# Seven PSUM banks shared with the side work in halved lumps, and a gelu whose VectorE instruction reads one SBUF operand

## The chip, the cores and the metric

The kernel runs on one core of a Trainium2 chip. The metric is the device time of one execution in microseconds, the median of the runs shown; lower is better. PE is TensorE, ACT ScalarE, DVE VectorE, POOL GpSimd; PEld is TensorE's weight load.

## What is computed

An adaLN block: 2048 tokens of width 512, 32 heads of width 16, then a token-shift MLP and a channel MLP with 1792 hidden columns. All in fp32.

```
h = layernorm(x) * (1 + ca) + sa
x = x + ga * (softmax(q k^T / 4) v) @ wo          # q, k, v = h @ wqkv, 32 heads
h = layernorm(x) * (1 + cb) + sb
t = gelu(layernorm(h) @ w1); t = shift(t, +1, -1, +2, -2 by quarters)
x1 = h + t @ w2
x = x + gb * (x1 + gelu(layernorm(x1) @ w3) @ w4)  # gelu: the tanh form
```

## The kernel before

**Attention is the spine.** There are 64 units, each a pair of heads (j = 0, 1) against one chunk of 512 queries, and 16 steps in a unit, one for each 128 keys. For each half step PE does a row pair: a score matmul (`sc`, L865) and a matmul for the row maximum of a later unit (`mb`, L849), each into a PSUM bank of its own. DVE reduces `mb` to a maximum (L845); ACT takes the exponential of `sc` into the int32 tile `pt` (L861). The exponential is written as an integer whose two 16-bit halves are used as two fp16 numbers. The low half needs a scaling by 0.5, one instruction over 128x1024 for each step (`p_low`): L909 on POOL, and in every eighth step (`LACT`) L907 on ACT. Then PE multiplies by V into `pv` (L924), two matmuls for the high half and two for the low half of each step.

**Blocks.** The rows and columns are written out in blocks of three half steps (`GRP`): six row matmuls, then the six `pv` matmuls of the block two before (`LAG`). So the scaling of a step has about two blocks until PE needs it. The block that finds its banks not yet drained waits on PE.

**Side work.** Between blocks PE does lumps of everything else: in units 0 to 15 the projections of q, k and v, and the splitting of the MLP weights into a high and a low part ("pieces": ACT copies to the high part, L750, DVE subtracts for the low part, L751); in units 16 to 63 the MLP of the 512 tokens that the 16 units before have finished ("tail", three of them beside attention; the fourth runs after it). All fp32 products are three matmuls of high and low parts (L298, L300, L302). A planner, `Sched`, runs while the program is built: it keeps an estimated time for each engine, gives each block a budget of side work, and puts an instruction of a side chain on ACT, DVE or POOL where it sees room. Nothing of it is left on the chip but the order: each engine executes its own list in order and waits for semaphores. `BMAX` caps a lump.

**PSUM.** Eight banks: one for `pv`, six in rotation for `sc` and `mb` (`NSM`), and one, `d0`, for all side work. (Before the main loop three of the six are lent to the side work.)

**The gelu** of the tails (L1187 to L1206) on a bank of 128x256 or 128x128: ACT copies half of the bank to `xs` (L1200) and squares it to `sq` (L1193), which frees the bank; DVE multiplies `(sq + 1/a) * xs` (L1201); ACT takes tanh (L1202); DVE multiplies `(tanh + 1) * xs` (L1203); ACT copies the high part (L1204); POOL subtracts for the low part (L1205). Both DVE instructions read two SBUF tiles. A tail has 36 of them: 8 of w1, 28 of w3.

Of the kernel before, what the change touches and what calls it, by code (L numbers as in the profile page):

```python
# [21 lines left out]
P = 128  # L22
# [18 lines left out]
BMAX = 1600.0  # L41
# [8 lines left out]
NSM = 6  # L50
LEND = 3
LENDS = -4
GRP = 3
LACT = 8
# [14 lines left out]
class Sched:  # L69
# [28 lines left out]
    def chain(self, *ops, prio=1, ready=None, bank=None):  # L98

        if ready is None:  # L100
            ready = self.T["P"] + PX
        n = 0
        while n < len(self.chains) and self.chains[n][2] <= prio:
            n += 1
        self.chains.insert(n, [ready, list(ops), prio, bank is not None and id(bank.tensor)])
# [18 lines left out]
    def misc(self, e, until):  # L124

        while True:
# [11 lines left out]
            ch = best[1]  # L138
            _, cost, fn = ch[1].pop(0)
            self.late = 0.0  # L140
            end = self.put(e, cost, ch[0], fn)
            if ch[1]:
                n = ch[1][0][0]
                ch[0] = max(end + (0 if n == e else XP[e] if n is None else XX), self.late)
            else:
                self.chains.remove(ch)
# [48 lines left out]
    def banks(self, n):  # L195
        self.avail, self.back, self.owner = list(range(n)), [], {}
        self.lent = None

    def return_banks(self, fn):

        self.lent = fn
        for i in self.avail:
            if i:
                fn(i, self.T["P"])
        for i, t in self.back:
            if i:
                fn(i, t)
        self.avail = [i for i in self.avail if not i]
        self.back = [x for x in self.back if not x[0]]

    def take(self, tile):

        i = self.avail.pop(0)
        b = tile(i)
        self.owner[id(b.tensor)] = i
        return b

    def free(self, b):

        i = self.owner.pop(id(b.tensor), None)  # L220
        if i and self.lent:
            self.lent(i, self.end + 200)
        elif i is not None:
            self.back.append((i, self.end + 200))
# [22 lines left out]
class Slots:  # L247
# [22 lines left out]
def kernel(ctx, tc, A_x, A_wqkv, A_wo, B_w1, B_w2, B_w3, B_w4, c, w_mod, out):  # L270
# [81 lines left out]
    def dbank(n):  # L352
        return sch.take(lambda i: psd["d"].tile([P, CH], F32, name=n, tag=f"s{NSM - i}" if i and psd["s"] else f"d{i}", bufs=1))
# [375 lines left out]
    def pieces_gen():  # L729
        while True:  # L730
# [15 lines left out]
            def store(i=i, c=c, w=w, f=f, gone=gone):  # L746
                for h, t in enumerate((w.bitcast(F32), f)):
# [3 lines left out]
                      ("D", cD(), lambda f=f, t=t, w=w: dve.tensor_tensor(t, f, w, op=OP.subtract)),  # L751
# [81 lines left out]
    def max_part(m, j):  # L833
# [6 lines left out]
        ready, sm.t[x] = sm.t[x], 1e9  # L840
# [10 lines left out]
    def score_part(s, j):  # L851
# [5 lines left out]
        ready, sm.t[x] = sm.t[x], 1e9  # L857
        r = slice(64 * j, 64 * j + 64)

        def after(e):  # L860
            ea = sch.crit("A", 500, e + PX, lambda: act.activation(pt[s][:, j], b, AF.Exp))  # L861
# [39 lines left out]
    def p_low(s):  # L901
# [4 lines left out]
        if s % LACT == LACT - 1:  # L906
            e_low[s] = XP["A"] + sch.crit("A", 945, ready, lambda: act.activation(o, i, AF.Copy, scale=0.5))  # L907
# [138 lines left out]
    def tail(ci):  # L1046
# [140 lines left out]
        def gelu(b, n, hi, lo, key):  # L1187
# [8 lines left out]
            def end():  # L1196
                done.add(key)
                live.remove(key)

            sch.chain(("A", cA(n), lambda: act.activation(xs, b, AF.Copy, scale=0.5)), ("A", cA(n), square),  # L1200
# [141 lines left out]
    for k, blk in enumerate(blocks + [[]] * LAG):  # L1342
        if LENDS in blk:
            sch.return_banks(lambda i, t: sm.t.__setitem__(NSM - i, t))
        if 0 in blk:
            while any(sch.owner.values()):
                sch.step()
# [9 lines left out]
        t, start = CIN, 0.0  # L1357
        banks = sorted(sm.t)
# [9 lines left out]
        sch.gap(start)  # L1368
        sch.T["P"] = max(sch.T["P"], start) + CIN
# [20 lines left out]
    while ("att", NC - 1) not in done:  # L1390
        sch.step()
# [41 lines left out]
```

## Time and profile before

| | |
|---|---|
| median of 3 runs | 2235.69 us (2226.3 to 2235.8) |
| the profiled execution, its own time | 2238.01 us |
| its span in the trace | 2236.1 us |
| mean granted clock of TensorE | 0.975 of full speed |
| PE, DVE, ACT, POOL busy | 94%, 80%, 72%, 67% of the span |

Attention begins at about 110 us and ends at about 2068 us; before it lies the first layernorm, behind it the fourth tail. The four stages of 16 units each take some 500 us: the first from 112 to 560 in the windows below, then one tail each. An instruction's "idle before" is time in which its engine had nothing to execute, with what ended it. PE's busy time counts matmuls until their modelled ends, so a PE at 97% can still start a block late.

### The profile page before, as it was taken

The numbers are of one execution on the slowest core, as the hardware profiler recorded it, in microseconds if no ns is written. First come the engines' busy times: TensorE is split into PE (matmuls) and PEld (weight loads), VectorE is DVE, ScalarE is ACT, GpSimd is POOL, SyncE is SP. The second block draws the span as 40 slices with busy tenths as digits, with TensorE's granted clock in tenths as the row PEclk, the third lists the DMA queues.
The fourth block names the chain that finished last, engine by engine and source line by source line (L and its number), as shares of the span: only waits on it lengthen the run. The fifth ranks groups of instructions, "written<-read, shape, count | busy, mean of one in ns | idle before, by whom it ended". The sixth has DMA issues, their size and how long they took to land.

```text
span 2236.1 us, 37341 instructions
## 1 busy us (share of the span) xinstructions
PE 2109.6 (94%) x12400; PEld 1181.3 (53%) x12400; DVE 1785.1 (80%) x3064; ACT 1615.7 (72%) x3254; POOL 1504.0 (67%) x1421
## 2 busy tenths in 40 slices
PE   6889999999999999999999999999899999999799
PEld 5544555554445555554445555555444555554688
DVE  6768887778998888888898888888798888884553
ACT  6467886667877777777868778777677877778353
POOL 3356776568966776667767877677678866768342
PEclk9889999998999999999999999999999999999999
DMA  5788887547644345446343344444524452443332
GB/s 196 197 253 254 218 231 208 154 142 204 178 140 118 113 104 149 112 112 182 75 111 91 98 109 135 126 111 97 163 75 111 112 149 80 126 112 114 132 131 81
DMA packets 201713, 313.37 MB, mean 140 GB/s; under 512 B 85520, under 2 KB 137232, under 8 KB 177296
## 3 DMA queue, kind: packets, MB, share of 16 engines
q1 hardware_dynamic: 201520, 310.98, 49.2%
q8 instruction: 99, 1.62, 0.3%
q14 instruction: 94, 0.77, 0.1%
HBM read 243.27 MB, written 67.11 MB: 139 GB/s over the span
## 4 chain that ended last, share of the span: by engine, by line
PE 59%; DVE 23%; ACT 8%; DMA 4%; issue 3%; POOL 2%; SPq 1%; POOLq 0%; ACTq 0%; DVEq 0%
PE pv L924 15%; DVE mx L845 14%; PE mb L849 10%; PE sc L865 8%; PE w L298 6%; PE w L300 5%; PE w L302 5%; ACT pt L861 3%; ACT pt L907 2%; DVE xs L1203 2%; DVE sq L1201 2%; DMA vst<-Vs 1%; DMA kst<-Ks 1%; DVE tst L309 1%; PE ot L949 1%
## 5 line engine op out<-in xcount | busy, mean ns | idle before, releaser
L909 POOL TENSOR_SCALAR pt<-pt 128x1024 f16<-128x1024 uint16 x896 | 1210.4, 1376 | 436.8 <-ACT pt L861 428.0
L845 DVE TENSOR_REDUCE mx<-mb 128x1 f32<-128x512 f32 x2048 | 1281.3, 681 | 220.9 <-PE mb L849 201.4
L861 ACT ACTIVATE pt<-sc 128x512 int32<-128x512 f32 x2048 | 1082.3, 607 | 272.3 <-PE mb L849 230.1
L849 PE MATMUL mb<-kst,qtl 48*128 48x512 f32 x2048 | 754.3, 457 | 46.8 <-DVE mx L845 27.8
L865 PE MATMUL sc<-qtl,kst 64*128 64x512 f32 x2048 | 726.7, 447 | 8.1 <-DVE mx L845 3.9
L924 PE MATMUL pv<-pt,vst 128*64 128x512 f16 x4096 | 614.2, 403 | 26.9 <-ACT pt L907 13.8
L849 PEld LDWEIGHTS mb<-kst,qtl 48*128 48x128 f32 x2048 | 352.8, 196 | 225.4 <-DVE mx L845 142.0
L865 PEld LDWEIGHTS sc<-qtl,kst 64*128 64x128 f32 x2048 | 339.4, 189 | 160.1 <-ACT pt L861 56.1
L924 PEld LDWEIGHTS <-vst 128*64 128x64 bf16 x4096 | 182.1, 109 | 335.1 <-issue 260.4
L298 PE MATMUL w<-A,wr 128*128 128x256 f32 (+2 forms) x576 | 178.5, 310 | 5.5 <-ACT A L292 3.0
L1205 POOL TENSOR_TENSOR g<-xs,g 128x256 fp32r<-128x256 f32 (+2 forms) x144 | 104.9, 731 | 115.2 <-ACT g L1204 115.0
L907 ACT ACTIVATE pt<-pt 128x1024 f16<-128x1024 uint16 x128 | 175.7, 1373 | 0.0
L300 PE MATMUL w<-A,wr 128*128 128x256 f32 (+2 forms) x576 | 168.4, 292 | 1.5 <-DVE A L288 1.3
L302 PE MATMUL w<-A,wr 128*128 128x256 f32 (+2 forms) x576 | 168.7, 293 | 0.0
L298 PEld LDWEIGHTS w<-A,wr 128*128 128x128 f32 x576 | 110.8, 192 | 56.4 <-ACT pt L861 24.6
L1203 DVE SCALAR_TENSOR_TENSOR xs<-sq,xs 128x256 f32<-128x256 f32 (+2 forms) x144 | 105.1, 734 | 37.6 <-ACT sq L1202 34.3
L1201 DVE SCALAR_TENSOR_TENSOR sq<-sq,xs 128x256 f32<-128x256 f32 (+2 forms) x144 | 110.4, 768 | 20.0 <-ACT sq L1193 18.9
L1200 ACT ACTIVATE xs<-w 128x256 f32<-128x256 f32 (+2 forms) x144 | 55.5, 386 | 92.9 <-PE w L302 92.0
L298 PE MATMUL w<-wr,g 128*128 128x512 f32 x288 | 121.6, 422 | 0.5 <-issue 0.5
L300 PE MATMUL w<-wr,g 128*128 128x512 f32 x288 | 119.1, 414 | 0.0
L302 PE MATMUL w<-wr,g 128*128 128x512 f32 x288 | 117.2, 407 | 0.3 <-POOL g L1205 0.3
L302 PEld LDWEIGHTS w<-A,wr 128*128 128x128 f32 x576 | 111.2, 193 | 9.5 <-issue 9.5
(124 smaller groups left out, 2015.0 us busy)
## 6 DMA issues: line engine op xcount, KB each, us to landing
wr<-Ws SPq DMA_DIRECT2D x80, 1024.0 KB, 5.2
vst<-Vs SPq DMA_DIRECT2D x62, 1024.0 KB, 6.3
kst<-Ks SPq DMA_DIRECT2D x126, 384.0 KB, 6.8
Vs<-vt SPq DMA_DIRECT2D x32, 512.0 KB, 4.9
qtl<-Qs SPq DMA_DIRECT2D x128, 96.0 KB, 4.8
Ws<-wq SPq DMA_DIRECT2D x40, 256.0 KB, 4.4
Ws<-wst SPq DMA_DIRECT2D x40, 256.0 KB, 3.8
wst<-in_B_w_dram SPq DMA_DIRECT2D x36, 256.0 KB, 4.4
```

The source lines that it names most:

```text
L298: te.matmul(o, lh, rh, start=first, stop=False)
L300: te.matmul(o, lh, rl, start=False, stop=False)
L302: te.matmul(o, ll, rh, start=False, stop=last)
L845: end = sch.crit("D", 605, e + PX, lambda: dve.reduce_max(mxs[u][:, j, g, c:c + 1], b, axis=AX.X))
L849: return ready, lambda: te.matmul(b, lhs, kst[u % 3][r, c * CH:(c + 1) * CH], start=True, stop=True), after
L861: ea = sch.crit("A", 500, e + PX, lambda: act.activation(pt[s][:, j], b, AF.Exp))
L865: return ready, lambda: te.matmul(b, kst[u % 3][r, kt * P:(kt + 1) * P], qst[u][r], start=True, stop=True), after
L907: e_low[s] = XP["A"] + sch.crit("A", 945, ready, lambda: act.activation(o, i, AF.Copy, scale=0.5))
L909: e_low[s] = XP["G"] + sch.crit("G", 1345, ready, lambda: pool.tensor_scalar(o, i, 0.5, 1.0, op0=OP.mult, op1=OP.mult))
L924: te.matmul(pv[u][64 * j:64 * j + 64, :], v[:, kt, i, 64 * j:64 * j + 64], p[:, j, 1 - i::2], start=(kt == 0 and i == 0), stop=(kt == NKT ...
L1201: ("D", cD(n), lambda: dve.scalar_tensor_tensor(sq, sq, 1.0 / GELU_A, xs, op0=OP.add, op1=OP.mult)),
L1203: ("D", cD(n), lambda: dve.scalar_tensor_tensor(xs, sq, 1.0, xs, op0=OP.add, op1=OP.mult)),
```

## The change

Four things change.

1. **Banks.** `NSM` is 7: `sc`, `mb` and the side work take any of seven banks (`share`, `take`); `d0` is gone. From unit 0 on the side work may hold two at a time (`MOST`), of which one may still be written (`open`). Ahead of a block `flush` emits the draining chains of banks that the block will need.
2. **Lumps.** `BMAX` falls from 1600 to 800 planned ns. Over the 64 units the PE order has 568 lumps between rows and columns in place of 524.
3. **The gelu** of the first three tails: ACT squares and copies the bank, unscaled; DVE multiplies `(sq + 1/a) * bank`, reading one SBUF tile and the bank, and only then is the bank free; ACT tanh; ACT `0.5 t + 0.5`; POOL multiplies `xs * sq`; then the high and low parts as before. One DVE instruction less, one more on ACT and on POOL. The fourth tail keeps the old gelu.
4. **Who scales and splits.** The pieces' subtraction moves from DVE to POOL (40 instructions of 128x512). The scaling of the low half goes to ACT only where the planner sees POOL over 800 ns behind ACT, and then as two instructions of 128x512: 17 steps of 1024 in place of 128.

The counts in the changed program: the old DVE pair remains 22 times for 128x256 and 14 times for 128x384 (both in the fourth tail); the new DVE instruction stands 94 times for 128x256 and 14 times for 128x128. POOL has 1007 scalings in place of 896.

```diff
-BMAX = 1600.0
+BMAX = 800.0
...
-NSM = 6
-LEND = 3
+NSM = 7
+MOST0 = 4
+MOST = 2
...
-LACT = 8
+LACT = 800.0
...
+    def share(self, slots, most):
+        self.avail, self.back, self.owner = [], [], {}
+        self.slots, self.most = slots, most
     def take(self, tile):
-        i = self.avail.pop(0)
+        if self.slots:
+            i = self.slots.take()
+            self.slots.t[i] = LATE
+        else:
+            i = self.avail.pop(0)
         b = tile(i)
         self.owner[id(b.tensor)] = i
+        self.open = id(b.tensor)
         return b
...
     def room(self, n=1):
+        if self.slots:
+            return self.open is None and len(self.owner) < self.most and min(self.slots.t) <= self.T["P"]
...
+    def flush(self, n):
+        for ch in list(self.chains):
+            while self.slots.late() > len(self.slots.t) - n and ch[1] and ch[3] in self.owner:
+                self.emit(ch)
...
             sch.chain(*ops, ("A", cA(), lambda f=f, w=w: act.activation(w, f, AF.Copy)),
-                      ("D", cD(), lambda f=f, t=t, w=w: dve.tensor_tensor(t, f, w, op=OP.subtract)),
+                      ("G", cG(), lambda f=f, t=t, w=w: pool.tensor_tensor(t, f, w, op=OP.subtract)),
...
-        if s % LACT == LACT - 1:
-            e_low[s] = XP["A"] + sch.crit("A", 945, ready, lambda: act.activation(o, i, AF.Copy, scale=0.5))
+        g, a = [max(sch.T[e], ready) for e in "GA"]
+        if g > a + LACT:
+            for h in range(2):
+                c = slice(h * CH, (h + 1) * CH)
+                e_low[s] = XP["A"] + sch.crit("A", 690, ready, partial(act.activation, o[:, c], i[:, c], AF.Copy, scale=0.5))
...
+            if psd["s"]:
+                def square_copy():
+                    act.activation(sq, b, AF.Square)
+                    act.activation(xs, b, AF.Copy)
+                    sch.T["A"] += cA(n)
+                def cube():
+                    dve.scalar_tensor_tensor(sq, sq, 1.0 / GELU_A, b, op0=OP.add, op1=OP.mult)
+                    sch.free(b)
+                sch.chain(("A", cA(n), square_copy), ("D", cD(n), cube),
+                          ("A", cA(n), lambda: act.activation(sq, sq, AF.Tanh, scale=GELU_A * GELU_C)),
+                          ("A", cA(n), lambda: act.activation(sq, sq, AF.Copy, scale=0.5, bias=0.5)),
+                          ("G", cG(n), lambda: pool.tensor_tensor(xs, xs, sq, op=OP.mult)), *tail_ops, bank=b)
+                return
...
-        if 0 in blk:
-            while any(sch.owner.values()):
-                sch.step()
...
+        need = sum((s >= 0) + (s + LEAD < NS) for s, _ in row)
+        sch.flush(need)
...
         sch.gap(start)
+        sch.flush(need)
```

What stands in the queues, at the first gelus of w3 in the second tail. On DVE, before: L845 is the maximum of a row, L1201 and L1203 are the gelu's two.

```order
L1201 SCALAR_TENSOR_TENSOR sq<-sq,xs 128x256
L845 TENSOR_REDUCE mx<-mb 128x1 x3
L1201 SCALAR_TENSOR_TENSOR sq<-sq,xs 128x256
L1203 SCALAR_TENSOR_TENSOR xs<-sq,xs 128x256 x2
L845 TENSOR_REDUCE mx<-mb 128x1 x5
L1201 SCALAR_TENSOR_TENSOR sq<-sq,xs 128x256
L845 TENSOR_REDUCE mx<-mb 128x1 x3
L1203 SCALAR_TENSOR_TENSOR xs<-sq,xs 128x256
L845 TENSOR_REDUCE mx<-mb 128x1 x3
L1201 SCALAR_TENSOR_TENSOR sq<-sq,xs 128x256
```

On DVE, in the changed kernel, at the same gelus: L863 is the maximum, L1232 the gelu's one, which reads the bank `w`.

```order
L1232 SCALAR_TENSOR_TENSOR sq<-sq,w_16235 128x256
L863 TENSOR_REDUCE mx<-mb 128x1 x8
L1232 SCALAR_TENSOR_TENSOR sq<-sq,w_16318 128x256
L863 TENSOR_REDUCE mx<-mb 128x1 x3
L1232 SCALAR_TENSOR_TENSOR sq<-sq,w_16420 128x256
L863 TENSOR_REDUCE mx<-mb 128x1 x6
L1232 SCALAR_TENSOR_TENSOR sq<-sq,w_16464 128x256
L863 TENSOR_REDUCE mx<-mb 128x1 x3
```

Of the two instructions a gelu one is left, and three to eight maxima stand between one gelu and the next; the old pairs stood back to back in places. On POOL, before: L909 scales a step, L1205 subtracts for a gelu.

```order
L909 TENSOR_SCALAR pt<-pt 128x1024 x4
L1205 TENSOR_TENSOR g_15929<-xs,g_15929 128x256
L909 TENSOR_SCALAR pt<-pt 128x1024 x2
L1205 TENSOR_TENSOR g_15929<-xs,g_15929 128x256 x2
L909 TENSOR_SCALAR pt<-pt 128x1024 x4
L1205 TENSOR_TENSOR g_16274<-xs,g_16274 128x256
```

On POOL, in the changed kernel: L931 scales, L1238 is the gelu's product, L1223 its subtraction.

```order
L931 TENSOR_SCALAR pt<-pt 128x1024 x2
L1223 TENSOR_TENSOR g_16011<-xs,g_16011 128x256
L931 TENSOR_SCALAR pt<-pt 128x1024 x3
L1238 TENSOR_TENSOR xs<-xs,sq 128x256
L931 TENSOR_SCALAR pt<-pt 128x1024
L1223 TENSOR_TENSOR g_16011<-xs,g_16011 128x256
L931 TENSOR_SCALAR pt<-pt 128x1024 x3
L1238 TENSOR_TENSOR xs<-xs,sq 128x256
L931 TENSOR_SCALAR pt<-pt 128x1024
L1223 TENSOR_TENSOR g_16011<-xs,g_16011 128x256
L1238 TENSOR_TENSOR xs<-xs,sq 128x256
```

There a gelu comes to four scalings with two instructions beside them, where it had one beside two to four. On ACT, before, at two gelus a little later in the same tail: L861 is the exponential, L907 the scaling on ACT, L1200, L1193, L1202 and L1204 the gelu's.

```order
L1202 ACTIVATE sq<-sq 128x256
L861 ACTIVATE pt<-sc 128x512 x3
L907 ACTIVATE pt<-pt 128x1024
L1204 ACTIVATE g_16274<-xs 128x256
L1200 ACTIVATE xs<-w_16579 128x256
L1193 ACTIVATE sq<-w_16579 128x256
L861 ACTIVATE pt<-sc 128x512 x3
L1202 ACTIVATE sq<-sq 128x256
L861 ACTIVATE pt<-sc 128x512 x3
L1204 ACTIVATE g_16274<-xs 128x256
```

On ACT, in the changed kernel: L879 is the exponential, L1227, L1228, L1236, L1237 and L1222 the gelu's square, copy, tanh, scaled copy and high part.

```order
L1227 ACTIVATE sq<-w_16589 128x256
L1228 ACTIVATE xs<-w_16589 128x256
L1236 ACTIVATE sq<-sq 128x256
L879 ACTIVATE pt<-sc 128x512 x3
L1237 ACTIVATE sq<-sq 128x256
L879 ACTIVATE pt<-sc 128x512 x3
L1227 ACTIVATE sq<-w_16673 128x256
L1228 ACTIVATE xs<-w_16673 128x256
L1236 ACTIVATE sq<-sq 128x256
L1222 ACTIVATE g_16419<-xs 128x256
L879 ACTIVATE pt<-sc 128x512 x3
```

The long scaling is gone from between the exponentials; the gelu has five short instructions where it had four.

## Rows read from the trace of the kernel before

**Rows 1.** The page: busy time, share and instructions of each engine over the span.
```profile
PE 2109.6 (94%) x12400; PEld 1181.3 (53%) x12400; DVE 1785.1 (80%) x3064; ACT 1615.7 (72%) x3254; POOL 1504.0 (67%) x1421
```

**Rows 2.** The page: chain that ended last, shares of the span by engine and line.
```profile
PE 59%; DVE 23%; ACT 8%; DMA 4%; issue 3%; POOL 2%; SPq 1%; POOLq 0%; ACTq 0%; DVEq 0%
PE pv L924 15%; DVE mx L845 14%; PE mb L849 10%; PE sc L865 8%; PE w L298 6%; PE w L300 5%; PE w L302 5%; ACT pt L861 3%; ACT pt L907 2%; DVE xs L1203 2%; DVE sq L1201 2%; DMA vst<-Vs 1%; DMA kst<-Ks 1%; DVE tst L309 1%; PE ot L949 1%
```

**Rows 3.** Windows by stage: length, busy us of each engine, clock, DMA share, GB/s.
```profile
111.80:560.00 448.20, 425.31 (x2434) 225.46 (x2434) 347.91 (x581) 331.00 (x632) 296.55 (x251) 0.95 0.73 208
560.00:1065.00 505.00, 483.28 (x2904) 255.07 (x2902) 437.01 (x738) 383.12 (x788) 369.66 (x346) 0.98 0.49 133
1065.00:1565.00 500.00, 486.66 (x2973) 257.44 (x2969) 431.86 (x743) 389.03 (x790) 376.89 (x344) 1.00 0.41 107
1565.00:2065.00 500.00, 475.61 (x2859) 252.58 (x2859) 406.66 (x686) 379.08 (x769) 360.90 (x338) 0.99 0.42 117
```

**Rows 4.** Timeline, start and length in us: end of a lump, start of a block.
```profile
1444.43 1.36 POOL L909 TENSOR_SCALAR pt<-pt 128x1024 f16<-128x1024 uint16 x1
...
1444.95 0.28 PE L302 MATMUL w<-A,wr 128*128 128x256 f32 x1
...
1445.07 0.28 PE L298 MATMUL w<-A,wr 128*128 128x256 f32 x1
...
1445.10 0.90 DVE L1203 SCALAR_TENSOR_TENSOR xs<-sq,xs 128x256 f32<-128x256 f32 x1
...
1445.31 0.28 PE L302 MATMUL w<-A,wr 128*128 128x256 f32 x1
...
1445.52 0.51 PE L849 MATMUL mb<-kst,qtl 48*128 48x512 f32 x1
```

**Rows 5.** Waits over the span: who waited for whom, us, times, longest.
```profile
PEld mb L849 <- DVE mx L845: 142.0, 334, 4.9
...
PE mb L849 <- DVE mx L845: 27.8, 49, 4.4
...
PE pv L924 <- ACT pt L907: 13.8, 25, 1.3
```

**Rows 6.** Source L909: who waited for the scaling instructions on POOL.
```profile
L909 POOL TENSOR_SCALAR pt<-pt x896: 1322/1352/1830, 108.4 to 2070.3; 128x1024 f16<-128x1024 uint16 x180
...
  PE pv L924: 2.5, 4
```

**Rows 7.** Groups by form: count, busy us, mean ns, idle before them.
```profile
L909 POOL TENSOR_SCALAR pt<-pt 128x1024 f16<-128x1024 uint16 x896 | 1210.4, 1376 | 436.8 <-ACT pt L861 428.0 <-ACT mf L896 3.6 <-DMA Ws<-wst 1.3
...
L907 ACT ACTIVATE pt<-pt 128x1024 f16<-128x1024 uint16 x128 | 175.7, 1373 | 0.0
...
L1201 DVE SCALAR_TENSOR_TENSOR sq<-sq,xs 128x256 f32<-128x256 f32 x116 | 93.3, 805 | 10.5 <-ACT sq L1193 9.9
L1203 DVE SCALAR_TENSOR_TENSOR xs<-sq,xs 128x256 f32<-128x256 f32 x116 | 87.4, 757 | 28.0 <-ACT sq L1202 27.5 <-POOL g L1205 0.6
L1205 POOL TENSOR_TENSOR g<-xs,g 128x256 fp32r<-128x256 f32 x116 | 84.3, 729 | 91.4 <-ACT g L1204 91.1
...
L1202 ACT ACTIVATE sq<-sq 128x256 f32<-128x256 f32 x116 | 49.3, 427 | 38.8 <-DVE sq L1201 38.1
...
L751 DVE TENSOR_TENSOR wst<-wst,wq 128x512 fp32r<-128x512 f32 x40 | 44.8, 1121 | 4.8 <-ACT wq L750 4.6
...
L668 DVE TENSOR_TENSOR vr<-v,vt 128x256 f32<-128x256 f32 x32 | 13.4, 418 | 18.2 <-ACT vt L682 16.7 <-ACT mf L896 1.4
...
L1254 POOL TENSOR_TENSOR xb<-xb,gbrow 128x512 f32<-128x512 f32 x16 | 20.6, 1286 | 0.9 <-ACT xn L1132 0.9
...
L1203 DVE SCALAR_TENSOR_TENSOR xs<-sq,xs 128x128 f32<-128x128 f32 x14 | 8.1, 581 | 1.2 <-ACT g L1204 0.7 <-ACT sq L1202 0.4
```

**Rows 8.** Source L1201: duration ns min, median, max of all its forms.
```profile
L1201 DVE SCALAR_TENSOR_TENSOR sq<-sq,xs x144: 276/558/1578, 688.1 to 2225.7; 128x256 f32<-128x256 f32 x116, 128x128 f32<-128x128 f32 x14, 128x384 f32<-128x384 f32 x14
```

**Rows 9.** Groups of ScalarE in 1065 to 1565 us.
```profile
L861 ACT ACTIVATE pt<-sc 128x512 int32<-128x512 f32 x543 | 287.1, 607 | 70.0 <-PE mb L849 63.0 <-PE sc L865 4.2 <-POOL nm L898 0.9
```

More of the change, by code (lines that the diff above doesn't have):

```diff
@@ L104, in chain @@
             n += 1
-        self.chains.insert(n, [ready, list(ops), prio, bank is not None and id(bank.tensor)])
+        bank = bank is not None and id(bank.tensor)
+        if bank == self.open:
+            self.open = None
+        self.chains.insert(n, [ready, list(ops), prio, bank])
     def put(self, e, cost, ready, fn):
@@ L137, in misc, with emit @@
                 break
[L138 to L146, printed above, removed]
+            self.emit(best[1])
+    def emit(self, ch):
+        e, cost, fn = ch[1].pop(0)
+        self.late = 0.0
+        end = self.put(e, cost, ch[0], fn)
+        if ch[1]:
+            n = ch[1][0][0]
+            ch[0] = max(end + (0 if n == e else XP[e] if n is None else XX), self.late)
+        else:
+            self.chains.remove(ch)
     def crit(self, e, cost, ready, fn):
@@ L220, in free @@
         i = self.owner.pop(id(b.tensor), None)
[L221 to L224, printed above, removed]
+        if i is not None:
+            if self.slots:
+                self.slots.t[i] = self.end + 200
+            else:
+                self.back.append((i, self.end + 200))
     def room(self, n=1):
+        if self.slots:
+            return self.open is None and len(self.owner) < self.most and min(self.slots.t) <= self.T["P"]
         for x in [x for x in self.back if x[1] <= self.T["P"]]:
@@ L254, in take, with late @@
         return min(range(len(self.t)), key=lambda i: self.t[i])
+    def late(self):
+        return sum(t == LATE for t in self.t)
 def cA(n=CH):
@@ L352, in dbank @@
     def dbank(n):
-        return sch.take(lambda i: psd["d"].tile([P, CH], F32, name=n, tag=f"s{NSM - i}" if i and psd["s"] else f"d{i}", bufs=1))
+        return sch.take(lambda i: psd["d"].tile([P, CH], F32, name=n, tag=f"s{i}" if psd["s"] else f"d{i}", bufs=1))
     qpx = ExitStack()
@@ L839, in max_part @@
         x, b = bank("mb")
-        ready, sm.t[x] = sm.t[x], 1e9
+        ready, sm.t[x] = sm.t[x], LATE
         r = slice(64 * j, 64 * j + 48)
@@ L1203, in gelu @@
                       ("D", cD(n), lambda: dve.scalar_tensor_tensor(xs, sq, 1.0, xs, op0=OP.add, op1=OP.mult)),
-                      ("A", cA(n), lambda: act.activation(hi, xs, AF.Copy)),
-                      ("G", cG(n), lambda: pool.tensor_tensor(lo, xs, hi, op=OP.subtract)),
-                      (None, 0, end), bank=b)
+                      *tail_ops, bank=b)
         def wait_bank():
@@ L1296, in tail @@
         done.add(("tail", ci))
-    sch.banks(1 + LEND)
-    sm.t[NSM - LEND:] = [1e9] * LEND
+    sch.share(sm, MOST0)
     sch.add(pieces_load(), 0)
@@ L1343 @@
         if LENDS in blk:
[L1344 to L1347 removed]
+            sch.most = MOST
         for x in blk:
@@ L1390 @@
     while ("att", NC - 1) not in done:
+        sch.step()
+    while sch.owner:
         sch.step()
```

20 lines of the change are left out of this document (7 added, 13 removed).

## The prediction

> **What bounds the kernel now.** I read the page's engine line first. PE is busy for 94% of the span and DVE for 80%, ACT 72%, POOL 67% [rows 1]. PE is the engine to fill; the question is what makes it start its blocks late. The chain that ended last answers by shares: 59% of it is PE, 23% DVE, 8% ACT, and only 2% POOL [rows 2]. Inside DVE's share 14% are the maxima of L845, and the two gelu instructions L1203 and L1201 stand with 2% each. ACT's long scaling L907 stands with 2%. So DVE and ACT are on the path through banks: a maximum or an exponential that is late keeps a bank, and PE's next block waits. The waits say the same: weight loads of `mb` waited 142.0 us in 334 places for a maximum, and its matmuls 27.8 us more [rows 5].
>
> POOL is not on that path. Its 896 scalings kept `pv` waiting for 2.5 us in 4 places [rows 6], while 128 scalings on ACT cost `pv` 13.8 us in 25 [rows 5]. The two blocks between a step's rows and its columns hide what POOL does late, and POOL sat idle for 436.8 us before L909, nearly all of it for exponentials [rows 7].
>
> By stage: in the three stages with a tail beside attention DVE is busy for 407 to 437 us of some 500, ACT for 379 to 389, POOL for 361 to 377, and PE for 476 to 487 [rows 3]. The clock is 0.98 to 1.00 there, so it is no term of the sum.
>
> Why DVE is so full: L1201 takes 805 ns in the mean for 128x256, L1203 757 [rows 7], but over all forms L1201 runs from 276 to 1578 ns [rows 8]. L1203 with 0.90 us ran wholly beside or behind a scaling on POOL that had begun 0.67 us before it and ended at 1445.79, 0.21 us before L1203's own end [rows 4]. L668, also a two-operand instruction of 128x256 but with one operand in a PSUM bank, takes 418 in the mean [rows 7]. I read this as DVE waiting for POOL where both operands lie in SBUF.
>
> **The change part by part.** *DVE.* The first three tails have 108 of the 144 gelus. L1203 goes: 94 x 0.757 + 14 x 0.581 = 79 us [rows 7]. L1201 becomes an instruction with one operand in the bank; the trace has no such gelu instruction. Its price lies between L668's 418 ns and L1201's own 805. I take 418, since that row has the same engine, size and operand places: 94 x (0.805 - 0.418) = 36 us less, and 0 at the other end. The 40 subtractions of the pieces go: 40 x 1.121 = 45 us [rows 7]. DVE loses 160 us.
>
> The Trainium skill, "SBUF — State Buffer", section "Who interferes with whom", says that a DVE instruction with two SBUF inputs contends with a GpSimd instruction that reads SBUF, and that one with at most one SBUF input does not. By that rule the new instruction costs what it costs alone, and the 36 us are all gained; if the stretching had another reason, they would not be. The spread in [rows 8] against L668's mean agrees with the rule so far.
>
> *ACT.* Out go 128 scalings, 175.7 us; in come 34 halves at half of 1373 ns, 23 us, and 94 scaled copies at L1202's 427 ns, 40 us [rows 7]; the 14 small ones add an estimated 4. ACT loses 108 us.
>
> *POOL.* 111 scalings more at 1.376 are 153 us; 94 products at the price of the subtraction L1205, 0.729, are 69 us, the 14 small ones an estimated 6; 40 subtractions at L1254's 1.286 are 51 us [rows 7]. POOL gains 279 us and goes from 1504 to 1783, which is 80% of the old span. In a tail stage it gets 32 scalings (44 us) and 36 products (26 us): 431 to 447 us in a stage of 500.
>
> *PE.* The matmuls are the same. A lump costs its switch: the starts of two side matmuls are 0.12 us apart, the last one's start and the next row's 0.21 [rows 4], so 0.09 us for each. The 44 lumps more cost 4 us.
>
> *Banks.* With one of seven under the side work the rows have six, as before; with none, seven. I set this at nothing. It is a gain where a side bank used to be waited for, and a loss where the gelu's bank, which now waits for DVE as well, is one of the six that the block needs (second rival).
>
> *The sum on the path.* 2% of 2236 us is 45 us, for each of L1203, L1201 and L907, between 34 and 56 by rounding [rows 2]. Of L1203's main form 94 of 116 go: 36 us. Of L1201's, 94 of 116 lose 48%: 18 us. Of L907 87% goes: 39 us. Together 93 us, if nothing is late instead.
>
> POOL is late next. Where gelus follow each other at three steps each, as in the changed DVE list, POOL needs 3 x 1.352 (the median, [rows 6]) + 2 x 0.729 = 5.51 us for them. The second tail stage did 543 exponentials, 271.5 steps, in 500 us [rows 9]: 1.84 us a step, 5.52 for three. So evenly paced gelu stretches can win nothing, while stretches that ran slower than the mean can. Of the 54 us of the gelu I keep half, 27; its ends are 0 and 54. L907's 39 us I keep for the three tail stages, 29. In the first stage I count nothing: DVE's 45 us and ACT's quarter are given, but POOL, at 297 of 448 us [rows 3], gets the 51 us of the pieces. Its ends are 10 us either way, the size of L907's quarter.
>
> 27 + 29 - 4 = 52 us. The profiled execution took 2238.0 us, 2.3 over the median of the runs; 2238.0 - 52 - 2.3 gives **2184 us**. Its own range, with half the rounding: 2155 to 2222.
>
> **The rivals.** *POOL's lag stays hidden.* For it: 2.5 us of waits for 896 scalings [rows 6]. Then the gelu's whole 54 us are won, and DVE's emptier queue shortens the waits of `mb` too: 2184 - 27 - 15 = 2142, down to 2110 with the shares rounded up. Against: POOL would be at 95% of such a stage.
>
> *The bank comes late.* The gelu's bank was free after two ACT instructions; now a DVE instruction follows, 0.42 us plus what stands ahead in DVE's list. At 0.42 us for each of 108 that is 45 us, and the gain is gone: 2229, no change. It decides where a block finds the side work with two banks; the emptying ahead of a block speaks against it, since it leaves one.
>
> *POOL holds the columns, slower.* POOL executes in order. The new product waits for ACT's scaled copy, the subtraction for ACT's high part, and all scalings stand behind them. L1205 waited 91.4 us for 116, 0.79 us each [rows 7]. If the new product does so too: 108 x 0.79 = 85 us at most; half of it, with nothing won from the gelu and 29 from L907, gives 2236 + 43 - 29 + 4 = 2254. It decides from where POOL has under 0.4 us to spare in three steps, and by the 5.51 against 5.52 it has none. Against it: an engine that is behind finds its inputs ready, and its waits shrink.
>
> The Trainium skill, "GPSIMD Engine Reference", section 4.1 "Engine selection", gives elementwise work to VectorE, since GpSimd is about twice as slow with two inputs. By it the move of 148 instructions to POOL is a loss, this last rival; the rows agree on the price (729 against 418 ns), not yet on who has time.
>
> *The new DVE instruction is stretched as well.* Then L1201's 18 us stay; this is inside the forecast's range.
>
> **How the numbers follow.** Forecast, 2155 to 2222: 0.59. Hidden lag, 2110 to 2155: 0.13. Late bank, 2222 to 2247: 0.12. POOL, 2225 to 2300: 0.16, a quarter of it within 0.5%. Half a per cent is 11 us and about what a measurement can tell from no change: faster means under 2224.5. Faster 0.73, within 0.5% 0.15, slower 0.12. The range 2115 to 2250 leaves out 0.12 above and some 0.03 below.
>
> **What would show it.** In the new profile: DVE busy near 1625 us, ACT near 1510, POOL near 1780; the new gelu instruction at 410 to 430 ns with little spread; no long scaling on ACT; fewer waits of `mb` for maxima than 142 us. Right about POOL: its idle time before the scalings falls from 437 us to 150 or less, and a few `pv` waits for it appear. The forecast is wrong if `pv` waits for POOL by tens of us (the third rival), if `mb` or `sc` wait for the gelu's DVE instruction (the second), or if POOL stays under 85% of a tail stage's time while the time falls below 2155 (the first).

## The result and the profile after

The changed kernel takes 2198.25 us in the median of four runs (2190.31 to 2199.29), against 2235.57 before (2226.3 to 2235.8). The ratio is 0.983, 95% interval 0.980 to 0.985: some 38 us faster. A second set gave 0.9822, 0.9805 to 0.9839. One execution of the change in that set took 3704 us and one of the kernel before in a later set 2292 us, and the ratios are taken without them. The forecast was 2184, so the direction and the range held and the gain came out at some three quarters of the 52 us of the sum.

The page of the changed kernel: the engines' busy time, and the chain that ended last by engine and by line. They answer to [rows 1] and [rows 2].

```profile
PE 2070.5 (95%) x12400; PEld 1162.6 (53%) x12400; DVE 1638.3 (75%) x2916; ACT 1533.1 (70%) x3268; POOL 1735.1 (79%) x1680
...
PE 67%; DVE 10%; POOL 7%; ACT 6%; DMA 6%; issue 3%; SPq 1%; POOLq 0%; ACTq 0%; DVEq 0%
PE pv L946 18%; PE mb L867 12%; PE sc L883 10%; PE w L320 7%; PE w L318 6%; PE w L316 6%; POOL pt L931 4%; DVE mx L863 4%; ACT pt L879 3%; DMA vst<-Vs 1%; SPq L93 1%; PE ot L971 1%; DMA wst<-in_A_wqkv_dram 1%; DMA wr<-Ws 1%; DMA kst<-Ks 1%
```

DVE's share of the chain fell from 23% to 10% and ACT's from 8% to 6%; POOL's rose from 2% to 7%, and PE's from 59% to 67%. The maxima (L863, before L845) have 4% of it where they had 14%, and neither a gelu instruction of DVE nor a scaling on ACT is left in the list. DVE is busy for 147 us less, ACT for 83 less, POOL for 231 more; the sum had 160, 108 and 279.

The groups of the changed kernel by form (count, busy us, mean ns, idle before), which answer to [rows 7]: the scaling on POOL, the new product, the pieces' subtraction, the new DVE instruction, the half scaling on ACT, and a DVE instruction that was not changed, of the layernorm.

```profile
L931 POOL TENSOR_SCALAR pt<-pt 128x1024 f16<-128x1024 uint16 x1007 | 1339.6, 1363 | 198.8 <-ACT pt L879 194.8 <-DMA qtl<-nm 0.9
...
L1238 POOL TENSOR_TENSOR xs<-xs,sq 128x256 f32<-128x256 f32 x94 | 69.5, 740 | 2.8 <-ACT sq L1237 2.3
...
L769 POOL TENSOR_TENSOR wst<-wst,wq 128x512 fp32r<-128x512 f32 x40 | 52.0, 1300 | 9.1 <-ACT wq L768 8.1 <-DMA vst<-Vs 0.8
...
L1232 DVE SCALAR_TENSOR_TENSOR sq<-sq,w 128x256 f32<-128x256 f32 x94 | 39.4, 420 | 60.6 <-ACT xs L1228 56.1 <-ACT mf L914 2.6 <-POOL pt L931 1.0
...
L114 ACT ACTIVATE pt<-pt 128x512 f16<-128x512 uint16 x34 | 24.2, 800 | 0.0
L1197 DVE SCALAR_TENSOR_TENSOR xb<-xb,trs,sbrow 128x512 f32<-128x512 f32 x16 | 22.7, 1416 | 1.3 <-POOL trs L1143 1.3
```

The new DVE instruction takes 420 ns in the mean, at the lower end of the bounds of 418 and 805. Its minimum, median and maximum over both of its forms, against 276, 558 and 1578 of L1201 in [rows 8]:

```profile
L1232 DVE SCALAR_TENSOR_TENSOR sq<-sq,w x108: 276/421/423, 664.5 to 1971.5; 128x256 f32<-128x256 f32 x94, 128x128 f32<-128x128 f32 x14
```

There is no spread left within a form (276 is the smaller one). POOL's idle time before the scalings fell from 436.8 to 198.8 us, not to the 150 or less that was expected. A half scaling on ACT has 800 ns in its row, but the records of the two halves of a pair overlap: 24.2 us for 17 pairs are 1.42 us a pair, where the sum had 2 x 687 ns.

Waits of the changed kernel, against [rows 5]:

```profile
POOL pt L931 <- ACT pt L879: 194.8, 257, 4.6
...
PEld mb L867 <- DVE mx L863: 43.2, 108, 4.8
...
PEld mb L867 <- DVE sq L1232: 34.1, 82, 0.8
...
PE pv L946 <- POOL pt L931: 25.2, 43, 1.1
```

The weight loads of `mb` waited 142.0 us for maxima; they wait 43.2. Two waits stand out: 34.1 us in 82 places for the gelu's DVE instruction, which holds a shared bank, and 25.2 us of `pv` for the scaling on POOL, where 2.5 had been for POOL [rows 6] and 13.8 for the scaling on ACT.

The windows of the changed kernel, as in [rows 3] (length, busy us of PE, PEld, DVE, ACT, POOL, clock, DMA share, GB/s):

```profile
111.80:560.00 448.20, 414.71 (x2483) 224.74 (x2482) 320.58 (x557) 321.15 (x641) 365.20 (x313) 0.97 0.77 219
560.00:1065.00 505.00, 486.75 (x3049) 255.25 (x3048) 414.94 (x735) 379.49 (x833) 444.96 (x433) 0.99 0.47 129
1065.00:1565.00 500.00, 487.54 (x2965) 255.40 (x2964) 399.89 (x705) 366.34 (x791) 432.44 (x415) 0.99 0.43 116
1565.00:2065.00 500.00, 477.47 (x2873) 262.59 (x2873) 364.33 (x656) 352.53 (x772) 407.60 (x406) 0.99 0.39 112
```

POOL is now busy for 408 to 445 us in a tail stage, the second engine after PE; the sum had 431 to 447.

The gain is not even over the stages. The exponentials that ACT did between 560 and 1065 us and between 1065 and 1565 us, in the changed kernel:

```profile
L879 ACT ACTIVATE pt<-sc 128x512 int32<-128x512 f32 x571 | 300.7, 600 | 98.8 <-PE mb L867 81.6 <-PE sc L883 12.8 <-POOL pt L931 1.6
```

```profile
L879 ACT ACTIVATE pt<-sc 128x512 int32<-128x512 f32 x536 | 282.3, 596 | 103.4 <-PE mb L867 86.5 <-PE sc L883 12.8 <-POOL pt L931 2.3
```

The same of the kernel before for the earlier window; for the later one it is [rows 9].

```profile
L861 ACT ACTIVATE pt<-sc 128x512 int32<-128x512 f32 x535 | 283.1, 608 | 68.0 <-PE mb L849 56.0 <-PE sc L865 9.6 <-POOL osb L960 0.4
```

In the second window 571 exponentials stand where 535 did. In the third, the window of [rows 9], 536 stand where 543 did.

These windows are cut by time, so in a faster kernel they hold later work. Cut by work, at the last exponential of units 15, 31, 47 and 63, one profiled execution of each kernel took (us; the last two kernels are experiments below):

| stretch | before | the change | the change, second set | before + gelu + rule | one side bank |
|---|---|---|---|---|---|
| to the end of unit 15 | 612.7 | 599.3 | 602.7 | 608.4 | 593.7 |
| units 16 to 31 | 484.7 | 463.5 | 464.0 | 465.0 | 480.7 |
| units 32 to 47 | 479.3 | 476.0 | 475.1 | 477.8 | 451.7 |
| units 48 to 63 | 493.4 | 481.9 | 484.0 | 478.1 | 465.0 |
| after unit 63 | 166.1 | 167.7 | 168.6 | 168.0 | 190.0 |

The three stages with a tail beside attention gained 21, 3 and 11 us. The stage of units 0 to 15, for which the sum counted nothing, gained 13 in this pair. The sizes are rough: the pair lies 48 us apart, more than the medians do, and the four profiled kernels that share the change's first stage took 599 to 608 us for it, the two that share the old one 612 and 613.

### The profile page after: what moved, and what is told of

The parts are those of the page before. It is cut to its first block, busy times and chain, and to the rows that moved or that the text cites. A ratio compares the mean times of both kernels' runs of the same rounds, so it can differ in the third digit from the quotient of the medians.

```text
span 2188.5 us, 37190 instructions
## 1 busy us (share of the span) xinstructions
PE 2070.5 (95%) x12400; PEld 1162.6 (53%) x12400; DVE 1638.3 (75%) x2916; ACT 1533.1 (70%) x3268; POOL 1735.1 (79%) x1680
## 4 chain that ended last, share of the span: by engine, by line
PE 67%; DVE 10%; POOL 7%; ACT 6%; DMA 6%; issue 3%; SPq 1%; POOLq 0%; ACTq 0%; DVEq 0%
PE pv L946 18%; PE mb L867 12%; PE sc L883 10%; PE w L320 7%; PE w L318 6%; PE w L316 6%; POOL pt L931 4%; DVE mx L863 4%; ACT pt L879 3%; DMA vst<-Vs 1%; SPq L93 1%; PE ot L971 1%; DMA wst<-in_A_wqkv_dram 1%; DMA wr<-Ws 1%; DMA kst<-Ks 1%
## 5 line engine op out<-in xcount | busy, mean ns | idle before, releaser
L863 DVE TENSOR_REDUCE mx<-mb 128x1 f32<-128x512 f32 x2048 | 1282.6, 682 | 295.9 <-PE mb L867 273.2
L931 POOL TENSOR_SCALAR pt<-pt 128x1024 f16<-128x1024 uint16 x1007 | 1339.6, 1363 | 198.8 <-ACT pt L879 194.8
L879 ACT ACTIVATE pt<-sc 128x512 int32<-128x512 f32 x2048 | 1078.1, 601 | 385.0 <-PE mb L867 322.3
L867 PE MATMUL mb<-kst,qtl 48*128 48x512 f32 x2048 | 722.0, 448 | 41.1 <-DMA kst<-Ks 9.2
L883 PE MATMUL sc<-qtl,kst 64*128 64x512 f32 x2048 | 693.9, 439 | 5.6 <-DVE sm L978 2.3
L946 PE MATMUL pv<-pt,vst 128*64 128x512 f16 x4096 | 610.7, 399 | 32.0 <-POOL pt L931 25.2
L867 PEld LDWEIGHTS mb<-kst,qtl 48*128 48x128 f32 x2048 | 341.3, 195 | 202.6 <-DVE mx L863 43.2
L883 PEld LDWEIGHTS sc<-qtl,kst 64*128 64x128 f32 x2048 | 334.4, 187 | 140.5 <-issue 45.0
L316 PE MATMUL w<-A,wr 128*128 128x256 f32 (+2 forms) x576 | 174.7, 303 | 3.0 <-ACT A L310 3.0
L318 PE MATMUL w<-A,wr 128*128 128x256 f32 (+2 forms) x576 | 175.9, 305 | 1.5 <-DVE A L306 1.3
L320 PE MATMUL w<-A,wr 128*128 128x256 f32 (+2 forms) x576 | 172.7, 300 | 0.0
L1223 POOL TENSOR_TENSOR g<-xs,g 128x256 fp32r<-128x256 f32 (+2 forms) x144 | 103.7, 721 | 81.1 <-ACT g L1222 80.7
L318 PEld LDWEIGHTS w<-A,wr 128*128 128x128 f32 x576 | 111.6, 194 | 37.0 <-issue 34.1
L316 PEld LDWEIGHTS w<-A,wr 128*128 128x128 f32 x576 | 111.8, 194 | 29.3 <-issue 18.3
L320 PEld LDWEIGHTS w<-A,wr 128*128 128x128 f32 x576 | 111.6, 194 | 23.7 <-issue 23.7
L1232 DVE SCALAR_TENSOR_TENSOR sq<-sq,w 128x256 f32<-128x256 f32 (+1 forms) x108 | 43.4, 403 | 71.3 <-ACT xs L1228 63.4
L1238 POOL TENSOR_TENSOR xs<-xs,sq 128x256 f32<-128x256 f32 (+1 forms) x108 | 75.9, 704 | 5.7 <-ACT sq L1237 5.2
L1143 POOL TENSOR_TENSOR trs<-tmv,mhalf 128x1 f32<-128x1 f32 x48 | 33.5, 701 | 54.1 <-DVE tmv L1140 54.1
```

Of the source, the lines that this page charges most:

```text
L316: te.matmul(o, lh, rh, start=first, stop=False)
L318: te.matmul(o, lh, rl, start=False, stop=False)
L320: te.matmul(o, ll, rh, start=False, stop=last)
L863: end = sch.crit("D", 605, e + PX, lambda: dve.reduce_max(mxs[u][:, j, g, c:c + 1], b, axis=AX.X))
L867: return ready, lambda: te.matmul(b, lhs, kst[u % 3][r, c * CH:(c + 1) * CH], start=True, stop=True), after
L879: ea = sch.crit("A", 480, e + PX, lambda: act.activation(pt[s][:, j], b, AF.Exp))
```

## The experiments

All ratios are to the kernel before, run on the same chip; one per cent is 22 us, and differences in us below are worked out from the ratios. The experiments ran in three sets on three chips; the kernel before had a mean granted clock of 0.974 in each. Theory A is the prediction's: relief of DVE by the gelu (27 us) and of ACT by the scaling rule (29 us). Theory B: POOL takes back what the gelu gives, and the gain is that of the banks and the short lumps.

| kernel | ratio | 95% interval | mean granted clock |
|---|---|---|---|
| the change | 0.9822 | 0.9805 to 0.9839 | 0.975 |
| without the new gelu | 0.9915 | 0.9899 to 0.9930 | 0.973 |
| without the scaling rule | 0.9940 | 0.9916 to 0.9964 | 0.975 |
| without the short lumps | 0.9893 | 0.9871 to 0.9914 | 0.974 |
| pieces on DVE | 0.9846 | 0.9822 to 0.9870 | 0.974 |
| gelu reading two SBUF tiles | 0.9862 | 0.9842 to 0.9881 | 0.973 |
| one side bank | 0.9792 | 0.9769 to 0.9814 | 0.971 |
| prices and pace | 0.9948 | 0.9928 to 0.9968 | 0.972 |
| before + new gelu | 0.9942 | 0.9919 to 0.9965 | 0.976 |
| before + scaling rule | 0.9990 | 0.9972 to 1.0007 | 0.974 |
| before + gelu + rule | 0.9832 | 0.9811 to 0.9853 | 0.982 |
| banks and lumps alone | 0.9942 | 0.9927 to 0.9957 | 0.974 |

A part of the scatter goes with the clock. The twelve executions of the kernel before with the scaling rule run from 2243.7 us at a clock of 0.966 to 2226.0 at 0.981, so 0.01 of the clock goes with some 12 us (an estimate from these two). Only one kernel, before + gelu + rule, lies far from the others in it.

### The change again, and without its gelu

> The change as it is, as the measure for the others. 2198 us of 2236 so far, a ratio of 0.983; both theories expect 0.981 to 0.985.

0.9822 (2197.27 us). This is the measure for the others.

```diff
-            if psd["s"]:
+            if False:
```

> The change with the old gelu (two VectorE instructions with two SBUF inputs) in all tails; the shared banks, the short lumps, the pieces on POOL and the scaling rule stay. Theory A (the gelu's relief of DVE is worth 27 us of the sum, the scaling rule 29): some 27 us slower than the change, ratio 0.995. Theory B (POOL takes back what the gelu gives DVE; the banks and lumps make the gain): ratio 0.981 to 0.986.

0.9915 (2219.49 us): 21 us slower than the change, interval clear of it. Theory B's 0.986 is outside. The gelu is worth 21 us in the company of the rest.

### The new gelu alone

The kernel before with the gelu of the change in its place; nothing else.

```diff
+            if psd["s"]:
+                ...
+                sch.chain(("A", cA(n), square_copy), ("D", cD(n), cube), ...
```

> The kernel before with the new gelu alone; one side bank, long lumps, every eighth scaling on ACT, pieces on DVE. Theory A: 27 us faster than before, ratio 0.988, new DVE instruction at 410 to 430 ns. Theory B: 0.998 or more.

0.9942 (2224.75 us): 13 us, between the two theories. The chain of this kernel by engine says why it is not more:

```profile
PE 64%; DVE 14%; ACT 12%; DMA 4%; issue 3%; POOL 2%; SPq 1%; ACTq 0%; POOLq 0%; DVEq 0%
```

DVE has gone from 23% to 14%, but ACT, which gets one instruction more for each gelu and keeps its long scalings, from 8% to 12%.

### Two SBUF tiles for the gelu's DVE instruction

```diff
-                    dve.scalar_tensor_tensor(sq, sq, 1.0 / GELU_A, b, op0=OP.add, op1=OP.mult)
+                    dve.scalar_tensor_tensor(sq, sq, 1.0 / GELU_A, xs, op0=OP.add, op1=OP.mult)
```

> The change, with the gelu's one DVE instruction reading the copy xs in SBUF in place of the bank, so both its inputs lie in SBUF; same instructions, same order, the bank is still held until it is done. If DVE waits for POOL only where both inputs lie in SBUF: this instruction's mean goes from 421 to about 800 ns with single ones over 1400, and the time rises by about 18 us, ratio 0.991. If the stretching had another reason: 421 ns and 0.983.

The instruction (minimum, median, maximum) with both inputs in SBUF:

```profile
L1232 DVE SCALAR_TENSOR_TENSOR sq<-sq,xs x108: 281/762/1531, 668.8 to 1985.4; 128x256 f32<-128x256 f32 x94, 128x128 f32<-128x128 f32 x14
```

Its median is 762 ns where it was 421, its maximum 1531 where it was 423. The instructions are the same and stand in the same places, so the stretching comes from where the second input lies. That it is POOL's doing shows in single executions. Of the 116 L1201 of 128x256 in the kernel before, the 27 during which POOL executed nothing took 407 to 427 ns, the 89 others 922 in the mean and up to 1578. In the change POOL was executing during 92 of the 94 L1232 of that size, and none took more than 423. By the rule of the Trainium skill, "SBUF — State Buffer", section "Who interferes with whom", that is the contention of VectorE and GpSimd for one read interface, and the trace agrees with it. The time is 0.9862 (2206.28 us), 9 us over the change (18 expected); the intervals just miss each other (0.9839 and 0.9842).

One thing besides the stretching differs, against what was expected of this edit: the bank is held for DVE in the planner's list alone. On the chip no matmul waits for the instruction any more; in the change, the first line here, weight loads of `mb` did. Who waited for L1232, first in the change, then with two SBUF tiles:

```profile
  PEld mb L867: 34.1, 82
...
  ACT sq L1236: 67.4, 87
```

So the 9 us are what the stretching costs less what the earlier bank gives back, and the stretching alone is not priced. The other 12 of the gelu's 21 us were not separated: one DVE instruction less, one more on ACT and on POOL.

### The scaling rule, taken out and alone

```diff
-        g, a = [max(sch.T[e], ready) for e in "GA"]
-        if g > a + LACT:
-            ...
+        if s % 8 == 7:
+            e_low[s] = XP["A"] + sch.crit("A", 945, ready, lambda: act.activation(o, i, AF.Copy, scale=0.5))
```

> The change with the old rule for the scaling: every eighth step whole on ACT (128 of 1371 ns), 896 on POOL. My sum set the rule at 29 us: 2226 us, 0.995. If the rule is worth nothing, since POOL's queue gets what ACT's loses: 0.982.

0.9940 (2223.51 us): 26 us slower than the change, near the 29 of the sum. It is also no faster than banks and lumps alone (0.9942, below): without the rule the new gelu adds nothing to them. The chain by engine:

```profile
PE 63%; ACT 12%; DVE 10%; POOL 6%; DMA 4%; issue 3%; SPq 1%; ACTq 0%; POOLq 0%; DVEq 0%
```

ACT stands at 12%, against 6% in the change. Now the same edit the other way round, put into the kernel before:

> The kernel before with the new scaling rule alone: ACT only where POOL is 800 planned ns behind, and in halves. By my sum 29 to 39 us faster: 0.983 to 0.987. If the long scalings on ACT were hidden: 0.998 to 1.002.

0.9990 (2232.15 us), no change. The 29 to 39 us are not there. The chain of this kernel by engine and by line, and its two gelu instructions on DVE (mean ns behind the busy time):

```profile
PE 57%; DVE 27%; DMA 5%; issue 3%; ACT 3%; POOL 3%; SPq 1%; POOLq 0%; DVEq 0%; ACTq 0%
DVE mx L845 16%; PE pv L928 15%; PE mb L849 10%; PE sc L865 8%; PE w L298 6%; PE w L300 5%; PE w L302 5%; DVE xs L1207 2%; DVE sq L1205 2%; POOL pt L913 1%; SPq L91 1%; ACT pt L861 1%; DMA vst<-Vs 1%; DVE tst L309 1%; DVE xb L1179 1%
```

```profile
L1205 DVE SCALAR_TENSOR_TENSOR sq<-sq,xs 128x256 f32<-128x256 f32 x116 | 99.0, 854 | 10.1 <-ACT sq L1197 9.5
L1207 DVE SCALAR_TENSOR_TENSOR xs<-sq,xs 128x256 f32<-128x256 f32 x116 | 90.2, 780 | 31.8 <-ACT sq L1206 31.2 <-POOL g L1209 0.6
```

The scaling did leave the path: ACT fell from 8% to 3%. But DVE rose from 23% to 27%. The two instructions take 854 and 780 ns in the mean where they took 805 and 757 [rows 7]: with more scalings on POOL, DVE waits for POOL longer. These two are 8.5 us busier for it in all, too little to explain the missing 29 to 39; the maxima L845 have 16% of the chain where they had 14%. What ACT gave up, DVE took, for the most part with work that had not changed.

### Gelu and rule together, without banks, lumps and pieces

The kernel before with both edits above.

```diff
-LACT = 8
+LACT = 800.0
...
-        if s % LACT == LACT - 1:
+        g, a = [max(sch.T[e], ready) for e in "GA"]
+        if g > a + LACT:
...
+                sch.chain(("A", cA(n), square_copy), ("D", cD(n), cube), ...
```

> The kernel before with the new gelu and the new scaling rule, nothing else. Alone they are worth 13 and 2 us. If they are independent: 15 us, 0.993. If the rule pays only where DVE no longer waits for POOL (the change loses 26 us without the rule): 0.985 to 0.988, with the new DVE instruction at 421 ns and no long scalings on ACT.

0.9832 (2196.41 us): 37 us, where the two alone make 13 and 2. Independence would have given 0.993, which is far outside. Some 9 of the 37 may be the clock's: its four executions had 0.980 to 0.984, the kernel before on the same chip 0.974 in the mean. Whether this kernel brings that clock about is not shown. 28 us would still be far from 15. The chain by engine, and two of its waits:

```profile
PE 68%; DVE 17%; ACT 5%; issue 3%; POOL 3%; DMA 2%; SPq 1%; POOLq 0%; DVEq 0%; ACTq 0%
```

```profile
PEld mb L849 <- DVE mx L845: 141.4, 370, 2.9
...
PE pv L928 <- POOL pt L913: 14.0, 22, 1.1
```

DVE 17% and ACT 5%: both fell, and PE has 68%. This kernel's time lies in the change's interval, although its weight loads still wait 141.4 us for maxima. So the fall of that wait from 142.0 to 43.2 us in the change is not the gelu's or the rule's doing, and it bought no more than some 11: 2 by the ratios and the 9 by which the clock may flatter this kernel.

### Banks and lumps

The change with the old gelu, the old scaling rule and the pieces on DVE.

```diff
-            if psd["s"]:
+            if False:
...
-        if g > a + LACT:
+        if s % 8 == 7:
...
-                      ("G", cG(), lambda f=f, t=t, w=w: pool.tensor_tensor(t, f, w, op=OP.subtract)),
+                      ("D", cD(), lambda f=f, t=t, w=w: dve.tensor_tensor(t, f, w, op=OP.subtract)),
```

> The change with the old gelu, the old scaling rule and the pieces on DVE: what is left are the seven shared banks and the lumps of 800. My sum: 1.000 to 1.002. If short lumps are worth by themselves what the change loses without them (15 us): 0.993.

0.9942 (2221.25 us): 13 us by themselves, where the sum had a loss of 4. One more edit is in them, which the list of four changes leaves out: the planner's price of an exponential, 480 ns in the change and all kernels made from it, 500 in the others. It was not tried alone. The weight loads' wait for maxima here:

```profile
PEld mb L867 <- DVE mx L863: 70.6, 175, 4.6
```

Half of what it was. Theory B has this much right: the banks and lumps do gain, on a kernel whose DVE and ACT are late. On top of the gelu and the rule they gain nothing that can be told apart (0.9832 against 0.9822), unless the 9 us of the clock are counted.

With this kernel the tie of gelu and rule can be seen a second time, at clocks of 0.973 to 0.975. Added to the banks and lumps, the gelu alone is worth nothing (0.9940), the rule alone 6 us (0.9915), both 27 (0.9822). Both together bring some 20 us more than the two alone, as on the kernel before, where it is 22. (The pieces differ too: here they are on DVE, in those three on POOL.)

```diff
-BMAX = 800.0
+BMAX = 1600.0
```

> The change with the old cap on a lump, 1600. My sum set the halving at 4 us of loss: 0.980 to 0.982. If short lumps are where the remaining gain comes from (19 us are left without the new gelu): 0.988 to 0.991.

0.9893 (2211.32 us): 16 us slower than the change, where the sum expected 4 faster. The cap matters with a shared pool, though it changes the number of lumps little: 552 with the old cap, 568 with the new, so most of the lumps are short in both. The kernel with the gelu, the rule, the old cap and the old pool was at 0.9832; that the shared pool with the old cap is a loss is not shown by this, since the clock (0.982 against 0.974), the pieces and the planner's price differ too. Two waits of this kernel:

```profile
PEld mb L867 <- DVE sq L1232: 39.4, 85, 2.4
...
PE pv L946 <- POOL pt L931: 28.4, 44, 1.3
```

They are 5 and 3 us larger than in the change, which doesn't account for 16. What the old cap costs in the shared pool stays open.

```diff
-MOST = 2
+MOST = 1
```

> The change with one bank at a time for the side work in place of two, still out of the seven. My sum set the banks at nothing: 0.980 to 0.986. If the second bank is what lets the side work go on while the first drains: 0.99 or more, with fewer lumps in the later stages and the side work running late.

0.9792 (2186.54 us), the fastest kernel of the study, 7 us under the change; the intervals overlap by a little (0.9805 to 0.9814), so that it beats the change is likely, not certain; its clock was the lower one, 0.971 against 0.975. The theory that the second bank lets the side work go on was wrong about the time and right about one sign: the side work runs late. After the last exponential this kernel does 884 matmuls of side work and 40 gelus, where the change does 794 and 36, and that stretch takes 190.0 us for 167.7. Three waits, and the exponentials of the third stage:

```profile
PEld mb L867 <- DVE mx L863: 101.6, 269, 4.6
...
PEld w L316 <- DVE sq L1232: 15.9, 37, 0.4
...
PE pv L946 <- POOL pt L931: 14.0, 19, 1.1
```

```profile
L879 ACT ACTIVATE pt<-sc 128x512 int32<-128x512 f32 x558 | 294.1, 602 | 84.3 <-PE mb L867 74.0 <-POOL pt L931 4.5 <-PE sc L883 3.1
```

No `mb` waits for the gelu's instruction among the long waits; the side work's own weight loads (`w`) wait for it, 15.9 us. And the third window, where the change won nothing, has 558 exponentials in 500 us against 536 and 543. Part of that is the late side work: in units 32 to 47 this kernel does 729 matmuls of it and 32 gelus, the change 802 and 36.

### The pieces

```diff
-                      ("G", cG(), lambda f=f, t=t, w=w: pool.tensor_tensor(t, f, w, op=OP.subtract)),
+                      ("D", cD(), lambda f=f, t=t, w=w: dve.tensor_tensor(t, f, w, op=OP.subtract)),
```

> The change with the subtraction of the pieces on DVE again (40 instructions). My sum set this at nothing, with 10 us either way: 0.978 to 0.987. It can only move the first stage, units 0 to 16.

0.9846 (2201.57 us): inside the range expected, and its interval overlaps that of the change. The pieces are worth nothing that can be told here.

### Truer prices, and a slower pace of the side work

```diff
-    return 2.2 * n + 40
+    return 2.2 * n + 175
...
-TAILB = (0.0, 500.0, 500.0, 540.0)
+TAILB = (0.0, 450.0, 500.0, 520.0)
...
-                e_low[s] = XP["A"] + sch.crit("A", 690, ready, partial(act.activation, ...
+                e_low[s] = XP["A"] + sch.crit("A", 790, ready, partial(act.activation, ...
```

> The change with POOL's planned price of a two-input instruction at the measured 738 ns for 128x256 in place of 603, ACT's half scaling at the measured 790 in place of 690, and the side work's budget at 450 and 520 in the second and fourth stage in place of 500 and 540, so that it reaches further into units 28 to 31, which are without. If the columns' 25 us of waits for POOL come from POOL's list being planned too full: 0.975 to 0.980, waits of the columns for POOL under 15 us. If they come from POOL's load itself: 0.982.

0.9948 (2221.9 us): a failure, 28 us slower than the change. The wait of the columns for POOL did not fall, and the first stage is behind; the exponentials up to 560 us in this kernel, then in the change:

```profile
PE pv L946 <- POOL pt L931: 26.5, 41, 1.3
```

```profile
L879 ACT ACTIVATE pt<-sc 128x512 int32<-128x512 f32 x446 | 234.7, 604 | 98.4 <-PE mb L867 87.1 <-PE sc L883 8.1 <-POOL pt L931 2.2
```

```profile
L879 ACT ACTIVATE pt<-sc 128x512 int32<-128x512 f32 x457 | 240.8, 607 | 89.9 <-PE mb L867 78.4 <-PE sc L883 5.6 <-POOL pt L931 4.4
```

26.5 us of waits against 25.2, and 446 against 457 exponentials. To the end of unit 15, where the budget is the old one, it took 615.4 us against 599 to 608 of the kernels with the change's first stage, so a part of the loss likely comes with the prices. Otherwise the three edits were not separated.

## Why the prediction was right, and where it was off

**What bounds the kernel: right.** DVE and ACT were late for PE's banks, POOL was not. Taking the gelu or the scaling rule out of the change costs 21 and 26 us, and the two without the rest reach 0.9832.

**The price of the new DVE instruction: right**, 420 ns for 418 taken, and for the reason given: with both inputs in SBUF it goes back to a median of 762, and where POOL executed nothing the old one took 407 to 427 too.

**The sum on the path: the step that failed.** It added the chain's 2% for each of L1203, L1201 and L907 as if each could be cashed by itself: 27 + 29 = 56 us after the deductions. Measured: gelu 13 alone, rule 2 alone, both 37 on the kernel before, and both 27 on top of the banks and lumps. The shares of a chain belong to one execution. Relieve ACT alone and the chain runs over DVE (8% to 3%, 23% to 27%); relieve DVE alone and it runs over ACT (23% to 14%, 8% to 12%). So some 20 us come only when both are relieved. They are in the 21 that the change loses without the gelu and again in the 26 that it loses without the rule; that these two lie near 27 and 29 does not bear the sum out.

There is a second tie, a smaller one: the scaling that leaves ACT goes to POOL, where it stretches the old gelu's DVE instructions, by 8.5 us of busy time. The sum had no term for it, though the row that says so stood in it: L1201 from 276 to 1578 ns. But a gelu that does not wait for POOL is not what makes the rule pay: with the rule and the stretched instruction the kernel was at 0.9862, with the unstretched one and no rule at 0.9940.

**What the number owes to luck.** The 56 us were for the three stages with a tail beside attention, which gained 34 to 36 in the profiled executions. Another 4 to 13 came in the first stage, where the sum had none, and banks and lumps did not cost the 4 that it took off. Errors of opposite sign put the time well inside the range.

**POOL's bound: not shown as the limit.** The sum said that evenly paced gelu stretches can win nothing, from 5.51 us of POOL work against 5.52 us of measured pace in the third window, and units 32 to 47 did gain only 3 us. But units 16 to 31, with as many gelus and 422 us of POOL's work for 433, gained 21. And with one side bank units 32 to 47 took 451.7 us with POOL busy for 426 of them, 94%, where the change has 91%. So POOL had room left in the change. What held that stage there stays open.

**Lumps: wrong sign.** Set at a loss of 4 us; within the change the lower cap is worth 16, and why is not known, for the count of lumps hardly moves. **Banks: not a nothing by themselves**, since with the lumps they are worth 13 us on a kernel with the old gelu and rule; a second side bank likely loses. On top of the rest the two came to nothing that can be told, so the errors hardly showed in the time. **Pieces: right**, within what can be measured.

**The rivals.** Hidden lag: no, POOL reached 88% of the second window and the gain stayed under the forecast. The late bank: its wait is there (34.1 us in 82 places), and with one side bank no `mb` or `sc` waits for the gelu's instruction, at a gain that the intervals do not quite settle; it did not cancel the change. POOL holding the columns: its wait is there too, 25.2 us of `pv`, where 13.8 for ACT and 2.5 for POOL had been; under the 43 us of that rival's price, and the gain outweighed it. Both waits were named as signs that the forecast is wrong, and both came while the forecast held: as signs they were too sharp.

## What to carry to other kernels

The shares of a chain of waits are not a price list: of two engines that stand on it in turn, relieving one hands its share to the other, and only both together pay (2 and 13 us alone, 37 together, some 9 of it perhaps the clock's; with shared banks 6 and nothing alone, 27 together). So what is lost by taking one part out of a finished change is not that part's own worth. When work is moved to POOL, look first for DVE instructions with two SBUF inputs that it will meet, and give these a bank as one input where one is at hand; the bank then waits for DVE. A wait that falls, as that of `mb` for maxima did from 142 to 43 us, proves no gain by itself: the fastest kernel kept 101.6 us of it.

## What the runs showed of the hardware

L1201 of 128x256, with two SBUF inputs on DVE, took 407 to 427 ns where POOL executed nothing meanwhile and 922 in the mean elsewhere. L1232 of that size, with one input in a bank, took 406 to 423 ns with POOL executing during 92 of 94. The unchanged layernorm instruction L1197, with SBUF inputs alone, went from 1194 to 1416 ns in the mean over its 16 executions: 742 to 752 ns in the 4 of before that met no work of POOL, 741 and 750 in the 2 of the change, and 1342 and 1512 in the mean in the others. Its row of before, in the groups by form:

```profile
L1175 DVE SCALAR_TENSOR_TENSOR xb<-xb,trs,sbrow 128x512 f32<-128x512 f32 x16 | 19.1, 1194 | 2.2 <-POOL trs L1121 2.2
```

Two scalings of 128x512 on ACT from 16-bit integers to fp16, one behind the other, took 1.42 us a pair, where one of 128x1024 took 1.37.
